# Pacing the last loads and stores of a fused linear-attention and FFN kernel, and moving five q chunks from TensorE transposes to DMA transposes

## The chip, the cores and the metric

The kernel runs on one core of one Trainium2 chip. The metric is the device time of one execution in microseconds (us). Every set of runs also contains runs of the kernel before, taken on the same chip. A run counts as slow when it is over 1.5% above the fastest run of the same kernel in its set; 2% is the threshold for "faster" or "slower".

## The reference

A linear attention with position-dependent features is followed by a feed-forward network (FFN) on all tokens. There are 8 batches, 8 heads, 576 positions and a head size of 64, so 4608 tokens of width 512.

```python
def phi(x, c, s):                       # 64 -> 128 features
    r = np.maximum(x, 0.0)
    return np.concatenate([r * c, r * s], axis=-1)
q_p, k_p = phi(q, cos_w, sin_w), phi(k, cos_w, sin_w)
kv  = np.einsum('bhsf,bhsd->bhfd', k_p, v)
z   = np.sum(k_p, axis=2)
num = np.einsum('bhsf,bhfd->bhsd', q_p, kv)
den = np.einsum('bhsf,bhf->bhs', q_p, z)[..., None] + 1e-06
x   = (num / den)                       # -> (4608, 512)
out = ((x @ w1) * (x @ w2) @ w3) @ w_out
```

## The kernel before

The kernel multiplies w3 and w_out once (`w34b`), and then works through the tokens in nine tiles of 512, t = 0 to 8. A tile is 24 *steps*, each of four wide matmuls: sixteen steps of products with w1 and w2, whose elementwise product is `abT`, and eight of output, which read it. The attention of later batches is slipped between these steps as narrow work. A batch has five chunks of rows. For each of them the kernel makes the q features, transposes them (`qpT`), multiplies them with `kvs` (called *num* here), normalizes the result (`xblk`), and transposes that into `xT`, which the FFN tile reads. So there are two transposes. Each can be done by TensorE, with a copy out of PSUM, or by a DMA that SP (SyncE) issues:

```python
def order_of(b):
    return [0, 1, 2, 3, 4] if b % 2 == 0 else [4, 0, 1, 2, 3]

def dma_q(b):                 # the q chunks that the DMA transposes
    return order_of(b)[5 if b < 2 else 2 if b == 2 else 0:]

def prep_q(b, c):
    features(b, feat_of(b)[1], raw[b, "q"], c)
    if c in dma_q(b):
        R = ROWS[c]
        nc.sync.dma_start_transpose(out=att_of(b)["qpT"][:, :, ds(columns_of(b, c), R)],
                                    in_=feat[b][1][:R, c].rearrange("p h f -> p (h f)"))
# ... (num, normalize) ...
def x_tr(b, c, by_vector=False, pst=None):
    # ...
    if b >= 2:
        nc.sync.dma_start_transpose(out=xT[t][:, :, ds(o, R)], in_=xf)
        return
    # ... else four transposes on TensorE and a copy
```

GpSimd issues the loads and most stores. The results of tiles 1 to 4 are held in SBUF in pairs of 512 KB, eight pairs, and stored in tiles 5 and 6. The other pairs are stored when they are made.

```python
held_pool.append(ctx.enter_context(tc.tile_pool(name="held", bufs=8)))

def store_held():
    osb, g = held.pop(0)
    store(nc.gpsimd, osb[:, :, :], g, 2)
# ... the plan of the tiles, cut:
    else:
        if t + 1 < B:
            attention_at(t + 1, slots, kv=(0, 1, 2, 3, 4), tr=(2, 4, 7, 10, 13),
                         nu=(6, 8, 10, 12, 14), xt=(6, 8, 10, 12, 14))
        for g in {5: (3, 9, 15, 20), 6: (1, 6, 11, 16)}.get(t, ()):
            slots[g].append(store_held)
        if t + 2 < B:
            spread(interleaved(t + 2), 0, 22, slots)
```

## Time and profile before

| | before |
|---|---|
| time, median of 3 | 251.24 us (251.13 to 251.31) |
| TensorE (PE) busy | 242.9 us of a span of 249.5 |
| VectorE (DVE), ScalarE (ACT), GpSimd (POOL) busy | 141.6, 124.5, 90.9 us |
| granted TensorE clock | full in every slice |
| waits of PE after 23 us | none listed |

The span is what the profiler sees of one execution; the device time is about 1.8 us longer. The prediction shows the lines of the page and reads them.

### The profile page before, as it was taken

What the parts mean: (1) busy time and instruction counts of PE and PEld (TensorE: products, weight loads), DVE (VectorE), ACT (ScalarE), POOL (GpSimd) and SP (SyncE); (2) the same over time, 40 slices, a digit from 0 to 9 for tenths busy, and PEclk for the clock granted to TensorE, in tenths of its full rate; (3) what the DMA queues carried; (4) which work ended last, traced back from release to release, by engine and by line L of the source; (5) the groups of instructions that cost most, each with busy time, mean ns of one, the idle gap of its engine ahead of it and who ended that gap; (6) DMA issues with size and microseconds to landing.
All of it is one profiled execution on the core that took longest, in us unless ns stands there. A gap on an engine that the chain in (4) does not pass through costs nothing.

```text
span 249.5 us, 4973 instructions
## 1 busy us (share of the span) xinstructions
PE 242.9 (97%) x1879; PEld 130.2 (52%) x1879; DVE 141.6 (57%) x338; ACT 124.5 (50%) x209; POOL 90.9 (36%) x171
## 2 busy tenths in 40 slices
PE   8899999999999999999999999999999999999994
PEld 3478555666555455545545554555455544444443
DVE  7876665657889628905980695189227704312321
ACT  2676325925966656555655555555432242323320
POOL 7754254540533612441433326280365040023000
PEclk9999999999999999999999999999999999999999
DMA  6999999999999999999999989999798992014013
GB/s 191 183 194 199 209 204 205 198 199 198 267 133 172 170 202 158 156 181 125 160 107 206 189 100 191 190 184 159 107 203 254 240 146 65 3 32 137 1 44 127
DMA packets 80760, 39.85 MB, mean 160 GB/s; under 512 B 48224, under 2 KB 77280, under 8 KB 80736
## 3 DMA queue, kind: packets, MB, share of 16 engines
q0 software_dynamic: 37024, 27.20, 72.0%
q1 hardware_dynamic: 43280, 11.87, 31.9%
q10 hardware_dynamic: 432, 0.46, 0.5%
q8 instruction: 15, 0.25, 0.4%
q14 instruction: 9, 0.07, 0.1%
HBM read 38.80 MB, written 9.44 MB: 193 GB/s over the span
## 4 chain that ended last, share of the span: by engine, by line
PE 92%; DMA 3%; DVE 1%; issue 1%; POOL 1%; ACT 0%; POOLq 0%
PE ffnps L462 50%; PE ffnps L508 24%; PE ffnps L230 6%; PE pnum L353 4%; PE pnum L295 4%; DMA qs<-in_q_dram 3%; PE pst L326 2%; PE pst L218 1%; PE pst L390 1%; PE ffnps L531 1%; POOL vs L112 0%; DVE xblk L363 0%; PE pfirst L353 0%; ACT xT L392 0%; DVE qp L263 0%
## 5 line engine op out<-in xcount | busy, mean ns | idle before, releaser
L503 DVE TENSOR_TENSOR abT<-asb,ffnps 128x512 bf16<-128x512 bf16 x68 | 46.5, 683 | 71.4 <-PE ffnps L462 70.6
L462 PE MATMUL ffnps<-xT,w1b 128*128 128x512 bf16 (+2 forms) x320 | 74.9, 357 | 0.4 <-ACT xT L392 0.2
L462 PE MATMUL ffnps<-xT,w2b 128*128 128x512 bf16 (+2 forms) x320 | 74.9, 357 | 0.0
L499 ACT CAST asb<-ffnps 128x512 bf16<-128x512 f32 x68 | 39.8, 586 | 61.6 <-PE ffnps L462 56.0
L508 PE MATMUL ffnps<-w34b,abT 128*128 128x512 bf16 x280 | 63.0, 379 | 0.0
L462 PEld LDWEIGHTS <-w1b 128*128 128x128 bf16 x320 | 29.4, 98 | 29.6 <-issue 0.6
L508 PEld LDWEIGHTS <-abT 128*128 128x128 bf16 x280 | 26.9, 98 | 31.1
L462 PEld LDWEIGHTS <-w2b 128*128 128x128 bf16 x320 | 26.8, 98 | 20.3
L267 ACT ACTIVATE qp<-qs,sinv 128x512 bf16<-128x512 bf16 (+2 forms) x40 | 28.3, 717 | 1.6 <-DMA qs<-in_q_dram 1.6
L363 DVE TENSOR_TENSOR xblk<-pnum,den 128x512 bf16<-128x512 f32 (+1 forms) x39 | 26.9, 691 | 1.4
L436 POOL DMA_DIRECT2D out_dram<-osb x20 | 10.6, 535 | 46.0 <-ACT osb L518 46.0
L287 POOL COPY va<-vs 128x512 bf16<-128x512 bf16 (+1 forms) x30 | 18.4, 624 | 18.7 <-PE pnum L295 8.9
L267 ACT ACTIVATE kp<-ks,sinv 128x512 bf16<-128x512 bf16 (+1 forms) x35 | 24.7, 721 | 0.0
L518 ACT COPY osb<-ffnps 128x512 f32<-128x512 f32 x19 | 11.1, 585 | 21.9 <-PE ffnps L508 21.9
L353 PEld LDWEIGHTS <-qpT 128*128 128x128 bf16 x320 | 15.1, 98 | 8.6 <-DVE qpT L340 0.6
L263 DVE TENSOR_SCALAR qp<-qs,cosv 128x512 bf16<-128x512 bf16 (+1 forms) x40 | 16.5, 418 | 0.7 <-DMA qs<-in_q_dram 0.6
L295 PEld LDWEIGHTS <-kp 128*128 128x128 bf16 x280 | 13.1, 98 | 7.1
L518 ACT COPY held<-ffnps 128x512 f32<-128x512 f32 x16 | 9.4, 586 | 14.3 <-PE ffnps L508 14.3
L353 PE MATMUL pnum<-kvs,qpT 128*128 128x65 bf16 x312 | 16.5, 194 | 0.0
L544 POOL COPY seen<-kp 128x1 bf16<-128x1 bf16 (+1 forms) x20 | 3.8, 188 | 33.9 <-DVE kp L263 26.1
L230 PE MATMUL ffnps<-woutb,w3T 128*128 128x512 bf16 x64 | 15.4, 379 | 0.0
L295 PE MATMUL pnum<-va,kp 128*128 128x65 bf16 x280 | 14.1, 193 | 0.0
(88 smaller groups left out, 195.3 us busy)
## 6 DMA issues: line engine op xcount, KB each, us to landing
out_dram<-held POOLq DMA_DIRECT2D x10, 256.0 KB, 6.3
qs<-in_q_dram POOLq DMA_DIRECT2D x8, 256.0 KB, 7.9
w3b<-in_moe_w_dram POOLq DMA_DIRECT2D x8, 256.0 KB, 12.8
ks<-in_k_dram POOLq DMA_DIRECT2D x6, 320.0 KB, 10.9
qs<-in_q_dram POOLq DMA_DIRECT2D x6, 320.0 KB, 8.6
vs<-in_v_dram POOLq DMA_DIRECT2D x6, 320.0 KB, 9.0
ks<-in_k_dram POOLq DMA_DIRECT2D x6, 256.0 KB, 8.2
vs<-in_v_dram POOLq DMA_DIRECT2D x6, 256.0 KB, 10.9
```

The costliest lines, as they stand in the source:

```text
L230: nc.tensor.matmul(acc[:, :], lhsT=w3T[:, lc, :], rhs=woutb[:, lc, :], start=(lc == 0), stop=(lc == 7))
L263: nc.vector.tensor_scalar(out=dst[:R, c, :, 0:D], in0=src[:R, :, c, :], scalar1=0.0, scalar2=cosv[:R, at:at + 1], op0=ALU.max, op1=ALU.mult)
L267: nc.scalar.activation(out=dst[:R, c, 0:n, D:F], in_=src[:R, 0:n, c, :], func=ACTF.Relu, scale=sinv[:R, at:at + 1], bias=0.0)
L287: eng.tensor_copy(out=feat_of(b)[2][:R, c, :, 0:D], in_=raw[b, "v"][:R, :, c, :])
L295: nc.tensor.matmul(kvt[:, h // 4, ds((h % 4) * 65, 65)], lhsT=kp[:, c, h, :], rhs=va[:, c, h, 0:D + 1], start=(i == 0 and h % 4 == 0), sto ...
L353: nc.tensor.matmul(nt[:, h // 4, ds((h % 4) * 65, 65)], lhsT=qpT[:, h, ds(at, 128)], rhs=kvs[:, h, :], start=True, stop=True)
L363: nc.vector.tensor_tensor(out=xblk[rows], in0=n4[:, :, :, 0:D], in1=den[rows].unsqueeze(3).to_broadcast([R, 2, 4, D]), op=ALU.mult)
L462: nc.tensor.matmul(out, lhsT=w[:, kc, ts(jc, 128)], rhs=x[:, kc, tok], start=(kc == 0), stop=(kc == 3))
L499: nc.scalar.copy(out=asb[:], in_=aT[:, :])
L503: nc.vector.tensor_mul(out=abT[:, jc, :], in0=asb[:], in1=bT[:, :])
L508: nc.tensor.matmul(ops[:, :], lhsT=abT[:, jc, ts(ms, 128)], rhs=w34b[:, jc, :], start=(jc == 0), stop=(jc == 7))
L518: nc.scalar.copy(out=osb[:, ms % 2, :], in_=ops[:, :])
```

## The change

The intent is to take five of the seven q chunks of batches 1 and 2 that TensorE still transposes over to the DMA, to give up one of the two raw buffers of q and v, and to pace all work of a batch on fixed steps, 25 steps apart. The SBUF that this frees holds twelve output pairs instead of eight. No pair is stored before the last batch: ten pairs are stored behind the steps of batch 7, each issued by GpSimd after it has read one column of what that step wrote, and six at fixed steps after that.

```diff
+    def raw_tile(name):
+        return ld.tile([P, H, NCH, D], BF16, name=name + "s", bufs=2 if name == "k" else 1)
@@
-        load(2, "kqv")
@@
-        return order_of(b)[5 if b < 2 else 2 if b == 2 else 0:]
+        return order_of(b)[5 if b == 0 else 2 if b == 1 else 0:]
@@
-        held_pool.append(ctx.enter_context(tc.tile_pool(name="held", bufs=8)))
+        held_pool.append(ctx.enter_context(tc.tile_pool(name="held", bufs=12)))
@@ (the old load_piece and interleaved are gone)
+    def behind(ap, *what):
+        seen = sm.tile([P, 1], BF16, name="seen", bufs=1)
+        nc.gpsimd.tensor_copy(out=seen[0:64, :], in_=ap)
+        if what:
+            load(*what)
+        else:
+            store_held()
@@ (behind_k, behind_q, behind_x: behind() of one column of k features, q features, x)
+    def plan_batch(b):
+        z = 28 + 25 * (b - 2)
         for i, c in enumerate(order_of(b)):
+            plan[z - 9 + 3 * i // 2].append(lambda c=c: prep_k(b, c))
+            if b + 1 < B and i in (0, 2):
+                plan[z - 9 + 3 * i // 2].append(lambda i=i: behind_k(b, i, b + 1, "k", i // 2))
+            plan[z - 5 + i].append(lambda c=c: prep_v(b, c))
+            g = z - (2 if b == 2 else 4) + 2 * i
+            plan[g].append(lambda c=c: prep_q(b, c))
+            if b == B - 1:
+                plan[g].append(lambda i=i: behind_q(b, i))
+            if b + 1 < B and i in (2, 4):
+                plan[g].append(lambda i=i: behind_q(b, i, b + 1, "v", i // 4))
+            plan[z + 1 + i].append(lambda c=c, i=i: kv_chunk(b, c, i))
+            plan[z + 7 + 2 * i].append(lambda c=c: num(b, c))
+            if b + 1 < B and i in (1, 3):
+                plan[z + 7 + 2 * i].append(lambda i=i: behind_x(b, i, b + 1, "q", i // 2))
+            if b == B - 1:
+                plan[z + 7 + 2 * i].append(lambda i=i: behind_x(b, i))
+            plan[z + 7 + 2 * i].append(lambda c=c: x_tr(b, c))
@@
+    for g in (170, 172, 174, 176, 192, 194):
+        plan[g].append(store_held)
@@ (batch 1)
-            attention_at(1, between, kv=(14, 14, 14, 14, 15), tr=(12, 13, 17, 18, 19),
-                         nu=(16, 17, 18, 20, 22), xt=(18, 19, 20, 22, 25))
+            attention_at(1, between, kv=(14, 14, 14, 14, 14), tr=(12, 13, 17, 18, 19),
+                         nu=(15, 17, 19, 20, 25), xt=(18, 20, 21, 22, 27))
+            for i in range(2):
+                between[11 + i].append(lambda i=i: behind_q(1, 2 + 2 * i, 2, "k", i))
+            for i, g in enumerate((15, 17, 17, 19)):
+                between[g].append(lambda i=i: behind_x(1, (i + 1) // 2, 2, "vvqq"[i], i % 2))
```

For batch 7, z is 153. Its q features and q transposes come at steps 149 to 157, each with a store behind it; its num and x at 160 to 168, again each with a store. Tile 7 begins at step 168.

More of the change, by code (lines that the diff above doesn't have):

```diff
@@ L108, with load_first @@
     raw = {}
-    def load_first(eng, t, src, c0=0, n=4, b=0):
-        rows = src[b, :, 0:512, :].rearrange("h (p j) d -> p h j d", j=4)
-        eng.dma_start(out=t[:, :, c0:c0 + n, :].rearrange("p h j d -> p h (j d)"),
-                      in_=rows[:, :, c0:c0 + n, :].rearrange("p h j d -> p h (j d)"))
+    def load_first(eng, t, src, c0=0, n=4, b=0, rows=slice(0, P)):
+        at = src[b, :, 0:512, :].rearrange("h (p j) d -> p h j d", j=4)
+        eng.dma_start(out=t[rows, :, c0:c0 + n, :].rearrange("p h j d -> p h (j d)"),
+                      in_=at[rows, :, c0:c0 + n, :].rearrange("p h j d -> p h (j d)"))
     def load_first4(eng, t, src, b=0):
         eng.dma_start(out=t[0:64, :, 4, :], in_=src[b, :, 512:S, :].rearrange("h p d -> p h d"))
+    def raw_tile(name):
+        return ld.tile([P, H, NCH, D], BF16, name=name + "s", bufs=2 if name == "k" else 1)
     def load(b, which, part=None):
@@ L121, in load @@
             if part != 1:
-                raw[b, name] = ld.tile([P, H, NCH, D], BF16, name=name + "s")
+                raw[b, name] = raw_tile(name)
             if b in own:
-                if part != 1:
-                    load_first(nc.gpsimd, raw[b, name], src, b=b)
-                if part != 0:
+                half = slice(64 * part, 64 * part + 64)
+                load_first(nc.gpsimd, raw[b, name], src, b=b, rows=half)
+                if part == 1:
                     load_first4(nc.gpsimd, raw[b, name], src, b=b)
@@ L149 @@
     k0 = raw[0, "k"] = wst.tile([P, H, NCH, D], FP32, name="kf", bufs=1)
-    q0 = raw[0, "q"] = ld.tile([P, H, NCH, D], BF16, name="qs")
-    v0 = raw[0, "v"] = ld.tile([P, H, NCH, D], BF16, name="vs")
+    q0 = raw[0, "q"] = raw_tile("q")
+    v0 = raw[0, "v"] = raw_tile("v")
     load_first(nc.sync, k0, k)
@@ L512, in ffn_groups @@
             if ms % 2 == 0:
-                if 1 <= t <= 4:
-                    osb = held_pool[0].tile([P, 2, 512], FP32, name="held")
-                else:
-                    pool = (fsb, held_pool[0])[ms // 2]
-                    osb = pool.tile([P, 2, 512], FP32, name="osb", bufs=1)
+                osb = held_pool[0].tile([P, 2, 512], FP32, name="held")
             nc.scalar.copy(out=osb[:, ms % 2, :], in_=ops[:, :])
@@ L520, in ffn_groups @@
                 store((nc.sync, nc.scalar)[ms % 2], osb[:, ms % 2:ms % 2 + 1, :], 4 * t + ms, 1)
-            elif ms % 2 == 1 and 1 <= t <= 4:
+            elif ms % 2 == 1:
                 held.append((osb, 4 * t + ms - 1))
-            elif ms % 2 == 1:
-                store(nc.gpsimd, osb[:, :, :], 4 * t + ms - 1, 2)
             yield
@@ L539, in prep_units @@
         return [(lambda f=f, c=c: f(b, c)) for f in parts for c in order_of(b)]
-    def load_piece(b, i, dst, c):
+    def behind(ap, *what):
         seen = sm.tile([P, 1], BF16, name="seen", bufs=1)
-        nc.gpsimd.tensor_copy(out=seen[0:ROWS[c], :], in_=dst[0:ROWS[c], c, 0, 0:1])
-        load(b, "kqv"[i // 2], i % 2)
-    def interleaved(b, pieces=range(5)):
-        units = []
-        for i, c in enumerate(order_of(b)):
-            units.append(lambda c=c: prep_k(b, c))
-            if b + 1 < B:
-                units.append(lambda c=c, i=i: load_piece(b + 1, pieces[i], feat[b][0], c))
-            units.append(lambda c=c: prep_q(b, c))
-            if b + 1 < B and i == NCH - 1 and pieces[i] < 5:
-                units.append(lambda c=c: load_piece(b + 1, 5, feat[b][1], c))
-            units.append(lambda c=c: prep_v(b, c))
-        return units
+        nc.gpsimd.tensor_copy(out=seen[0:64, :], in_=ap)
[3 more added lines that the diff above has]
+            store_held()
@@ new lines, in behind_k, with behind_q, behind_x @@
+    def behind_k(b, i, *what):
+        behind(feat[b][0][0:64, order_of(b)[i], 0, 0:1], *what)
+    def behind_q(b, i, *what):
+        behind(feat[b][1][0:64, order_of(b)[i], 0, 0:1], *what)
+    def behind_x(b, i, *what):
+        c = order_of(b)[i]
+        r = out_rows(b, c).start
+        behind(att[b]["x"][c][r:r + 64, 0, 0, 0:1], *what)
+    plan = [[] for _ in range(24 * NT)]
+    def plan_batch(b):
+        z = 28 + 25 * (b - 2)
+        for i, c in enumerate(order_of(b)):
+            plan[z - 9 + 3 * i // 2].append(lambda c=c: prep_k(b, c))
[15 more added lines that the diff above has]
+            plan[z + 7 + 2 * i].append(lambda c=c: x_tr(b, c))
@@ L594 @@
                                                      space=bass.MemoryType.PSUM)))
+    for b in range(2, B):
+        plan_batch(b)
+    for g in (170, 172, 174, 176, 192, 194):
+        plan[g].append(store_held)
     for t in range(NT):
@@ L611 @@
             between = [[] for _ in range(32)]
-            later = [[] for _ in range(24)]
             spread(prep_units(1, (prep_k,)), 6, 8, between)
@@ L615 @@
             spread(prep_units(1, (prep_v,)), 13, 13, between)
-            attention_at(1, between, kv=(14, 14, 14, 14, 15), tr=(12, 13, 17, 18, 19),
-                         nu=(16, 17, 18, 20, 22), xt=(18, 19, 20, 22, 25))
-            later[:8] = between[24:32]
+            attention_at(1, between, kv=(14, 14, 14, 14, 14), tr=(12, 13, 17, 18, 19),
+                         nu=(15, 17, 19, 20, 25), xt=(18, 20, 21, 22, 27))
+            later = between[24:32]
+            for i in range(2):
+                between[11 + i].append(lambda i=i: behind_q(1, 2 + 2 * i, 2, "k", i))
+            for i, g in enumerate((15, 17, 17, 19)):
+                between[g].append(lambda i=i: behind_x(1, (i + 1) // 2, 2, "vvqq"[i], i % 2))
             for jp in range(8):
@@ L627 @@
             slots[16].append(open_held)
-            slots[16].append(lambda: load(3, "kqv"))
-            spread(prep_units(2, (prep_k,)), 20, 23, slots)
         elif t == 1:
-            for g in range(24):
-                slots[g] += later[g]
-            spread(prep_units(2, (prep_q,)), 0, 4, slots)
-            spread(prep_units(2, (prep_v,)), 0, 4, slots)
-            attention_at(2, slots, kv=(2, 3, 4, 5, 6), tr=(3, 5, 7, 9, 11),
-                         nu=(8, 10, 12, 14, 16), xt=(8, 10, 12, 14, 16))
-            slots[4].append(lambda: load_piece(4, 0, feat[2][1], 3))
-            spread(interleaved(3, range(1, 6)), 6, 23, slots)
-        else:
-            if t + 1 < B:
-                attention_at(t + 1, slots, kv=(0, 1, 2, 3, 4), tr=(2, 4, 7, 10, 13),
-                             nu=(6, 8, 10, 12, 14), xt=(6, 8, 10, 12, 14))
-            for g in {5: (3, 9, 15, 20), 6: (1, 6, 11, 16)}.get(t, ()):
-                slots[g].append(store_held)
-            if t + 2 < B:
-                spread(interleaved(t + 2), 0, 22, slots)
+            for g, units in enumerate(later):
+                slots[g] += units
+        for g in range(24):
+            slots[g] += plan[24 * t + g]
         for g, _ in enumerate(ffn_groups(t)):
```

## The prediction

> **What bounds the kernel now.** I read the page first: its row of engines, the slices, and the chain of work that ended last.
>
> ```profile
> PE 242.9 (97%) x1879; PEld 130.2 (52%) x1879; DVE 141.6 (57%) x338; ACT 124.5 (50%) x209; POOL 90.9 (36%) x171
> ...
> PE   8899999999999999999999999999999999999994
> ...
> PEclk9999999999999999999999999999999999999999
> ...
> PE 92%; DMA 3%; DVE 1%; issue 1%; POOL 1%; ACT 0%; POOLq 0%
> ```
>
> TensorE is busy in every slice, at full clock, and 92% of the chain lies on it; the next engine, VectorE, is at 57%. But a PE that is "busy" may still be waiting inside, since the ends of its matmuls are modelled, so I checked two things. The waits of PE are these, all of them:
>
> ```profile
> PE unread L180 <- DVE zeros L156: 1.2, 1, 1.2
> PE kva L312 <- DVE va L287: 0.9, 1, 0.9
> PE ffnps L462 <- ACT xT L392: 0.2, 1, 0.2
> PE pst L339 <- DVE qp L263: 0.2, 1, 0.2
> PE ffnps L462 <- DVE xT L392: 0.2, 1, 0.2
> ```
>
> 2.7 us, all before 23 us. The second check is by start times in the timeline of PE, where the next start, not the duration, gives the cost:
>
> ```profile
> 47.06 1.03 PE L230 MATMUL ffnps<-woutb,w3T 128*128 128x512 bf16 x4
> 47.92 0.61 PE L326 MATMUL pst<-identb,qp 128*128 128x128 bf16 x8
> 48.37 1.03 PE L230 MATMUL ffnps<-woutb,w3T 128*128 128x512 bf16 x4
> ...
> 53.89 1.02 PE L508 MATMUL ffnps<-w34b,abT 128*128 128x512 bf16 x4
> 54.75 0.61 PE L326 MATMUL pst<-identb,qp 128*128 128x128 bf16 x8
> 55.25 0.43 PE L353 MATMUL pnum<-kvs,qpT 128*128 128x65 bf16 x8
> ...
> 59.92 0.39 PE L390 MATMUL pst<-identb,xblk 128*128 128x128 bf16 x4
> 60.14 0.42 PE L353 MATMUL pnum<-kvs,qpT 128*128 128x65 bf16 x8
> 60.40 1.89 PE L508 MATMUL ffnps<-w34b,abT 128*128 128x512 bf16 x8
> ```
>
> Four wide matmuls (one "step" of the FFN; a token tile has 24) cost 47.92-47.06 = 0.86 us. Eight transposes of q, one chunk, cost 48.37-47.92 = 0.45 us. Four of x cost 0.22, eight narrow matmuls (one chunk of kv or of num) 0.26 us. With these I recompute a stage. Tiles 2 to 6 last from 88.03 to 204.45 = 116.42 us, 23.28 each; the work is 24 x 0.864 = 20.74 plus ten narrow chunks at 0.255 = 2.55, together 23.29. Tiles 7 and 8 begin at 204.45 and 225.17, 20.72 apart, which is 24 x 0.864. So from 88 us to the end PE has no gap at all: nothing that moves loads, copies or stores about can gain there. It can only lose.
>
> **What the Trainium skill says.** "TensorE: Matmul & The Clock Gate", section "Part 4: PE-mode transpose", gives about 275 ns per 128x128 transpose in a kernel and names the copy out of PSUM that follows. The trace differs on what a transpose costs the stream: its row shows 219 ns each, but eight start within 0.45 us, 56 ns apiece; I use that. "PSUM — Partial Sum Buffer", section "Engine vs sequencer instructions": the queues of ScalarE, VectorE and GpSimd are strict FIFO. So a feature step that waits for its q load stands in front of the abT product behind it; the trace of before has only 0.6 us of such waiting on VectorE for q and does not test it. "DMA: Bandwidth & Descriptors", section "Issuing engines are not separate DMA queues": SP's transposes and GpSimd's loads interleave on the same 16 engines. The landing times of before fit that: x transposes take from 2.4 to 9.6 us, q transposes from 3.2 to 11.3.
>
> ```profile
> L385 SPq DMA_TRANSPOSE xT<-xblk x30: 1171/1218/3447, 75.3 to 199.3; - x30
> DMA to landing us min/median/max: 2.4/5.4/9.6
> ...
> L281 SPq DMA_TRANSPOSE qpT<-qp x28: 1194/1280/3884, 68.5 to 179.9; - x28
> DMA to landing us min/median/max: 3.2/6.2/11.3
> ```
>
> **The change part by part.** I counted the instructions on each engine in the order of both programs.
>
> (1) PE loses exactly 40 matmuls, 1879 to 1839, all of them q transposes: three chunks of batch 1 and two of batch 2, which now go through the DMA transpose. The first two chunks of batch 1 stay on PE. 5 x 0.445 = 2.2 us, wholly on the path, since three lie between 52.7 and 63.5 us and two in tile 1, both PE-bound. VectorE loses their five copies, 5 x 0.69 = 3.4 us, off the path.
>
> (2) The stage from 52.68 to 63.47 us is 10.79 us long. Its work: eight steps 6.91, five num chunks 1.28, three q chunks 1.33, x transposes 0.11 + 3 x 0.22 = 0.77, sum 10.29. So 0.5 us is small waits; by start times they are 0.09 us before the first num, 0.06 before the second, 0.10 before the first x transpose and 0.22 after it. In the changed order the transposes of q no longer share the two PSUM transpose buffers here, num of batch 1 begins at 15 instead of 16, and most num and x transposes have an FFN step of 0.86 us between them. I count 0.4 us of the 0.5 as gained. Tile 1 has another 24.56-24.41 = 0.15 us, of which I count nothing. One num chunk moves from tile 0 into tile 1: zero.
>
> (3) Loads. Batch 2 no longer loads at 40 to 47 us but behind the features and products of batch 1 (about 46 to 59 us); q and v have one raw buffer each. All later loads are spread over the tile. None is on PE; the gain is zero, the risk is under the rivals.
>
> (4) Twelve output pairs held (before eight), all sixteen pairs stored from step 149 on: ten behind the q features and x of batch 7, six at fixed steps. Same bytes, no PE work. The last two pairs go at steps 192 and 194, about where tile 7's stores ran before (201.9 to 226.6 us covers tiles 6 and 7), so the tail of the last tile, 244.16 to 249.5 us, stays.
>
> (5) GpSimd gets 47 one-column copies instead of 25, 22 more at 0.19 us = 4 us, on an engine at 36%: nothing.
>
> Sum: 251.24 - 2.2 - 0.4 = 248.6 us if no new wait appears.
>
> **The rivals.** *First, the x transposes come too late for their tile.* Before, tile t+1's batch had its products at steps 6 to 14 of tile t; now a batch is paced every 25 steps, and the x that a tile needs is produced only eight or nine steps ahead of it. For tile 3 the last needed num stands at step 64 and the tile begins at 72: seven steps and two num chunks, 7 x 0.864 + 2 x 0.26 = 6.6 us. For tiles 5 and 7 three chunks lie between: 6.8 us. For tiles 2, 4 and 6 there are nine steps, about 7.4, 7.7 and 8.0 us. From this comes off the normalization, 0.16 + 0.20 + 0.69 = 1.05 us, and some 0.3 us in VectorE's and SP's queues. That leaves 5.2 us against a median landing of 5.4: right on the edge. For it: the old maximum of 9.6 us. Against it: that median comes from x transposes queued between q transposes and loads; now q transposes end before the x begin, loads are paced singly, and 2.4 to 4 us should be usual. If each of tiles 2 to 7 stalled by 1 us, six tiles eat 6 us: 254.6. I expect one or two stalls of some tenths.
>
> *Second, the stores collide with batch 7.* Ten pairs of 512 KB start within steps 149 to 168, about 20 us, which is 5.2 MB or some 260 GB/s, with the transposes of q and x of batch 7 in the same time; the slices of before peak at 267 GB/s. The x that tile 7 waits for is issued at step 160, behind five pairs. If it lands in 8 us instead of 5, PE stalls 2 to 3 us once. Against it: queues interleave, and GpSimd itself waits when its transfers are outstanding (it waited 4.5 us in all for held stores before).
>
> *Third, q of batch 2.* Its second half is issued behind x of order 2, whose num ends by my sums at 57.0 us; plus 1.1 us of VectorE and GpSimd's two issues of 0.68, it leaves near 59 us. Its first feature stands at step 26, which PE reaches near 64.5 us. Loads took 4.5/7.9/11.6 us to land before; with the burst of 40 to 55 us gone I expect 5 to 7, so VectorE and ScalarE wait 0 to 1.5 us. PE can run some four steps on through the four FFN tiles in PSUM, so it stalls only if q lands after about 67.3 us: not likely, worth 0 to 1 us.
>
> *Fourth, a larger gain.* PE's work bounds it: with the start and tail kept, at most 2.2 us of work and the 0.65 us of waits just named go. 248.3 is the floor; 2% would need 246.2.
>
> **Range and chances.** Base 248.6; I add 0.4 us for the average of the first three rivals: 249.0. Low end 248.2, just under the floor for spread between runs (251.13 to 251.31 before). High end 250.9, where stalls cost 2.3 us over the base. For slower by over 2%, 256.3 us, stalls would have to reach 7.7 us, more than 1 us at every tile: 3%. Faster by over 2%: 1%. The rest within.
>
> **What would show it.** Right: PE with 1839 instructions, busy near 240 us; the stage of the eight output steps of tile 0 about 2 us shorter; PE's list of waits still under 4 us; tiles 2 to 6 still 23.3 us each. First rival: waits of L464 products on the transposes into xT at the starts of tiles, tiles longer than 23.3, and x landings near 5 us or more. Second: such a wait at tile 7 alone, with landings of x of 8 us and stores round it. Third: VectorE waiting for the load of qs near 65 us with a gap on PE near 68. My prediction is wrong if PE gets idle by more than 2 us in tiles 1 to 7, or if the stage around 53 to 63 us does not shrink.

## More of the kernel before

The features of batch t+2, with their q transposes, are made during tile t, a whole tile before their num. And x of batch t+1 is made at steps 6 to 14 of tile t, so the first x transpose has 18 steps (24 - 6), about 15.6 us, before tile t+1 reads it.

## The result, and the profile after

The changed kernel took 261.32 us (258.95 to 263.75), the kernel before 251.28 in the same set. Ratios in this document are the mean time of one kernel's fast runs over the mean of the other's in the same rounds, so they are not quite the ratio of the quoted medians. Here the ratio is 1.036 (95% interval 1.029 to 1.044): slower. The prediction was 249.0 us with a range of 248.2 to 250.9.

The profiled run of that set was the slowest of the four and counts as slow, so the same kernel was run once more (e10_changed_again below, 258.92 us for the profiled run, fast). Both profiles have the same stall at the same place; all detailed readings are from the fast one. This is the page of the slow one, its row of engines, slices of PE and of the clock, and the chain:

```profile
PE 243.6 (93%) x1839; PEld 127.7 (49%) x1839; DVE 142.9 (55%) x333; ACT 123.1 (47%) x209; POOL 95.7 (37%) x196
...
PE   8799999999999999999999999999998129999995
...
PEclk9999999999999999999999999999999757999999
...
PE 82%; DMA 13%; issue 2%; DVE 1%; POOL 1%; ACT 0%; POOLq 0%
```

PE did lose 40 matmuls, and the slices before the hole are nearly as full as before. Line numbers have moved by two: L464 is the product with w1 or w2, L510 the output, L355 num, L387 the DMA transpose of x. The hole takes about two slices of 6.5 us, the 32nd and 33rd; in them and in the next one the clock is granted at 0.5 to 0.7. The share of DMA in the chain has gone from 3% to 13%. The hole is the start of tile 7. The list of PE's waits in the fast profile (in all, times, longest) begins:

```profile
PE ffnps L464 <- issue: 5.7, 1, 5.7
PE pnum L355 <- DMA qpT<-qp: 1.5, 1, 1.5
```

In the slow profile the first two are 9.2 and 2.4 us. Here is PE's timeline of the fast profile at that place (start, duration, instruction, wait before it and what ended it):

```profile
203.42 0.43 PE L355 MATMUL pnum<-kvs,qpT 128*128 128x65 bf16 x8 [1.47 <-DMA qpT<-qp]
203.69 1.02 PE L510 MATMUL ffnps<-w34b,abT 128*128 128x512 bf16 x4
210.39 1.87 PE L464 MATMUL ffnps<-xT,w1b 128*128 128x512 bf16 x4 [5.68 <-issue]
212.05 0.65 PE L355 MATMUL pnum<-kvs,qpT 128*128 128x65 bf16 x8
212.51 1.72 PE L464 MATMUL ffnps<-xT,w2b 128*128 128x512 bf16 x4
214.06 1.03 PE L464 MATMUL ffnps<-xT,w1b 128*128 128x512 bf16 x4
```

A num waits 1.47 us for its transposed q. Then the first product of tile 7, which reads `xT`, waits 5.68 us. "Issue" means that the profile could not name what it waited for; SP's timeline of the same profile names it:

```profile
186.42 14.07 SPq L283 DMA_TRANSPOSE qpT<-qp  x5
200.59 14.55 SPq L387 DMA_TRANSPOSE xT<-xblk  x5
```

The first block of x was normalized by 197.4 us, but SP was still issuing q transposes until 200.49. The first x transpose was issued at 200.59 and landed after 9.7 us, the longest of its kind in this stretch, so at 210.3 us. PE goes on at 210.39.

After the hole, four wide matmuls take 212.05 - 210.39 = 1.66 us instead of 0.86, eight narrow ones 0.46 instead of 0.26, and four more wide ones 1.55; from 214.06 on it is 0.86 again. The half speed costs 0.80 + 0.20 + 0.69 = 1.7 us. The view by windows shows it (the columns after the window are its length, busy time and instructions of PE, PEld, DVE, ACT and POOL, then the clock, the DMA share and GB/s):

```profile
208.00:212.00 4.00, 1.61 (x4) 0.59 (x5) 0.00 (x0) 0.00 (x0) 1.06 (x2) 0.50 1.15 320
```

The clock is at 0.50 while the DMA engines move 320 GB/s. The Trainium skill, "TensorE: Matmul & The Clock Gate", section "What's actually happening", states that the clock falls to half after an idle window of about 3.4 us and comes back after about 3.4 us of sustained work. The trace agrees on the second figure: work resumes at 210.39 and the clock is whole again 3.7 us later. On the first it differs: PE is idle from 204.7 on, and in windows of 1 us the clock is down from 207 on, after 2.3 us. PE had also stood still for 1.47 us shortly before, so that it worked for only 1.3 of the 5.1 us up to the fall.

Where the time went, by the starts of the tiles in PE's timelines (us). The last column is the version of e1b_stores_away_gated below, which has the change without the stall:

| | before | changed (fast profile) | stores moved away |
|---|---|---|---|
| tile 1 begins | 63.47 | 62.22 | 61.75 |
| tile 2 begins | 87.87 | 86.44 | 85.97 |
| tile 6 begins | 181.00 | 179.88 | 179.53 |
| tile 7 begins | 204.28 | 210.39 | 202.55 |
| tile 8 begins | 225.00 | 233.05 | 223.52 |
| end of the span | 249.5 | 257.1 | 247.5 |

Up to tile 6 the change gained 1.12 us. Tile 6 then lasted 30.51 instead of 23.28 us; the difference of 7.23 is the two waits, 1.47 + 5.68 = 7.15. Tile 7 lasted 22.66 instead of 20.72, that is 1.94 more: 1.7 of half speed, and one num chunk of 0.26 that now lies in it. The last tile took 24.05 instead of 24.5 us, a gain of 0.45 that was not looked into.

### The profile page after: what moved, and what is told of

Read it like the earlier page. It is cut to its first block, busy times and chain, and to the rows that moved or that the text cites. A ratio compares the mean times of both kernels' runs of the same rounds, so it can differ in the third digit from the quotient of the medians.

```text
span 261.9 us, 4941 instructions
## 1 busy us (share of the span) xinstructions
PE 243.6 (93%) x1839; PEld 127.7 (49%) x1839; DVE 142.9 (55%) x333; ACT 123.1 (47%) x209; POOL 95.7 (37%) x196
## 4 chain that ended last, share of the span: by engine, by line
PE 82%; DMA 13%; issue 2%; DVE 1%; POOL 1%; ACT 0%; POOLq 0%
PE ffnps L464 47%; PE ffnps L510 18%; DMA qpT<-qp 10%; PE ffnps L232 5%; PE pnum L355 3%; PE pnum L297 3%; DMA qs<-in_q_dram 3%; PE pst L220 1%; PE pst L392 1%; PE pst L328 1%; PE ffnps L527 1%; DVE xblk L365 1%; POOL vs L112 0%; PE pfirst L355 0%; ACT xT L394 0%
## 5 line engine op out<-in xcount | busy, mean ns | idle before, releaser
L464 PE MATMUL ffnps<-xT,w1b 128*128 128x512 bf16 (+2 forms) x320 | 76.1, 362 | 9.5 <-issue 9.2
L464 PE MATMUL ffnps<-xT,w2b 128*128 128x512 bf16 (+2 forms) x320 | 75.8, 361 | 0.0
L510 PE MATMUL ffnps<-w34b,abT 128*128 128x512 bf16 x280 | 65.9, 379 | 0.0
L464 PEld LDWEIGHTS <-w1b 128*128 128x128 bf16 x320 | 29.1, 98 | 38.0 <-issue 11.8
L516 ACT COPY held<-ffnps 128x512 f32<-128x512 f32 x35 | 20.5, 585 | 51.9 <-PE ffnps L510 51.9
L464 PEld LDWEIGHTS <-w2b 128*128 128x128 bf16 x320 | 28.9, 98 | 27.2 <-issue 0.6
L510 PEld LDWEIGHTS <-abT 128*128 128x128 bf16 x280 | 25.5, 98 | 26.2
L438 POOL DMA_DIRECT2D out_dram<-held x42 | 22.1, 532 | 21.1 <-DMA out_dram<-held 10.4
L269 ACT ACTIVATE kp<-ks,sinv 128x512 bf16<-128x512 bf16 (+1 forms) x35 | 24.5, 721 | 0.0
L363 DVE TENSOR_SCALAR den<-pnum 128x8 f32<-128x8 f32 (+1 forms) x39 | 6.4, 165 | 32.7 <-PE pnum L355 32.7
L355 PEld LDWEIGHTS <-qpT 128*128 128x128 bf16 x320 | 15.0, 99 | 13.8 <-issue 3.7
L540 POOL COPY seen<-xblk 64x1 bf16<-64x1 bf16 x19 | 3.5, 185 | 46.4 <-DVE xblk L365 46.4
L265 DVE TENSOR_SCALAR qp<-qs,cosv 128x512 bf16<-128x512 bf16 (+1 forms) x40 | 18.7, 473 | 1.0 <-DMA qs<-in_q_dram 1.0
L355 PE MATMUL pnum<-kvs,qpT 128*128 128x65 bf16 x312 | 16.7, 195 | 2.6 <-DMA qpT<-qp 2.4
L289 POOL COPY va<-vs 128x512 bf16<-128x512 bf16 (+1 forms) x30 | 17.5, 630 | 0.0
L540 POOL COPY seen<-qp 64x1 bf16<-64x1 bf16 x17 | 3.3, 191 | 38.9 <-DVE qp L265 38.9
```

The lines of the kernel that those rows point to most:

```text
L265: nc.vector.tensor_scalar(out=dst[:R, c, :, 0:D], in0=src[:R, :, c, :], scalar1=0.0, scalar2=cosv[:R, at:at + 1], op0=ALU.max, op1=ALU.mult)
L269: nc.scalar.activation(out=dst[:R, c, 0:n, D:F], in_=src[:R, 0:n, c, :], func=ACTF.Relu, scale=sinv[:R, at:at + 1], bias=0.0)
L355: nc.tensor.matmul(nt[:, h // 4, ds((h % 4) * 65, 65)], lhsT=qpT[:, h, ds(at, 128)], rhs=kvs[:, h, :], start=True, stop=True)
L438: eng.dma_start(out=rows[:, :, cols], in_=osb[64 * i:64 * i + rows.shape[0], :, cols])
L464: nc.tensor.matmul(out, lhsT=w[:, kc, ts(jc, 128)], rhs=x[:, kc, tok], start=(kc == 0), stop=(kc == 3))
L510: nc.tensor.matmul(ops[:, :], lhsT=abT[:, jc, ts(ms, 128)], rhs=w34b[:, jc, :], start=(jc == 0), stop=(jc == 7))
```

## The experiments

The leading theory, called A in some of the texts: the pairs stored behind batch 7's q features and x delay, in the DMA engines, the transposes of q and x that batch 7 needs at once. Its main rivals: the lead of eight steps is too short in any case (then removing stores would not help, and an earlier batch 7 would); the late load of batch 2 or the single raw buffers do the harm; or, as a finer form of A, it is not the bytes that count but how packets of two queues take turns (T in the texts). Edits are against the changed kernel unless said otherwise.

### e1_stores_away: the stores after batch 7's transposes, first try

```diff
-            if b == B - 1:
-                plan[g].append(lambda i=i: behind_q(b, i))
...
-            if b == B - 1:
+            if b < B - 1 and i == 4:
                 plan[z + 7 + 2 * i].append(lambda i=i: behind_x(b, i))
...
-    for g in (170, 172, 174, 176, 192, 194):
+    for g in (170, 172, 174, 176, 178, 180, 182, 184, 186, 192, 194):
```

> The changed kernel with its stores moved, nothing else: five pairs go singly behind the last products of batches 2 to 6, the other eleven from step 170 on, when no transpose is left that a near product waits for. Theory A (the ten pairs stored beside batch 7 hold up its DMA transposes, and PE waits for them): the waits of 2.2 and 9.2 us at 204 to 215 us and the slow clock after them (about 2 us) go, and the first part's lead stays: 249 to 250.5 us. Rival B (the pace of 25 steps, with x made only eight steps ahead of tile 7, is too tight whatever else moves): a wait of several us stays at the start of tile 7, 255 us or more.

Measured: 263.54 us, ratio 1.039 (1.036 to 1.042). No faster than the changed kernel (ratios 1.036 and, in e10, 1.038): a miss. The cause is in the edit. The late stores had nothing to wait for, and a step number orders only the instructions of one engine; GpSimd, which had no other work, ran ahead and issued them in a burst. Its timeline shows this:

```profile
188.19 4.83 POOL L438 DMA_DIRECT2D out_dram<-held  x9
```

Instead of after 200 us they ran beside batch 7's q transposes, and PE waited again: in its profile (a slow run) 7.2 us at tile 7 and 6.3 us in four waits on `qpT`. What follows: the edit did not test what it was meant to. With stores again beside the transposes the stall was there, as A says; that the waits sum to more than in the changed kernel's slow profile (13.5 against 11.6 us) proves nothing, since the fast runs of the two do not differ.

### e2_half_stores: three pairs behind q, two behind x

```diff
-            if b == B - 1:
+            if b == B - 1 and i % 2 == 0:        # behind q features
...
-            if b == B - 1:
+            if b == B - 1 and i % 2 == 1:        # behind x
...
+    for g in (170, 172, 174, 176, 178, 180, 182, 184, 186, 192, 194):
```

> Five of the ten pairs stay beside batch 7 (behind q features 0, 2, 4 and products 1, 3), five go to steps after 170. Theory A, with lateness that grows with the stores in the way: landings of batch 7's last q transposes and first x transpose of some 6 to 9 us instead of 12.9 to 16.8, PE waits of 2 to 5 us in all instead of 11.4, 252 to 256 us. Rival B: no change beyond noise, about 260 us.

Measured: 249.70 us, ratio 0.993 (0.991 to 0.995). The stall is gone altogether: no wait of PE is listed after 59 us, and batch 7's q transposes landed in 3.2/4.3/7.3 us (minimum, median, maximum). This is better than I had expected; half the stores did not give half the stall, they gave none. The lead of eight steps was left as it was, so it is not too short by itself.

### e4_pe_last_batch: all stores in place, the critical transposes back on TensorE

```diff
     def dma_q(b):
+        if b == B - 1:
+            return order_of(b)[:3]
...
-        if b >= 2:
+        if b >= 2 and (b, c) != (B - 1, 4):                  # x transposes by DMA
...
-            plan[z + 7 + 2 * i].append(lambda c=c: x_tr(b, c))
+            if b == B - 1 and i >= 3:
+                plan[z + 2 * i - 1].append(lambda c=c: q_tr(b, c))
+            plan[z + (10 if b == B - 1 and i == 0 else 7 + 2 * i)].append(lambda c=c: x_tr(b, c))
```

> All stores where the changed kernel has them; only the three transposes of batch 7 with a near deadline (its last two q chunks, its first x block) go back to TensorE. Theory A says that PE stood still for late DMA transposes and nothing else: no wait over 1 us is left, 2 x 0.45 + 0.11 = 1.0 us of PE work comes back, 250 to 251.5 us. If instead the stores slow PE, VectorE or the buffers themselves (rival C), most of the 10 us stays: 257 us or more.

Measured: 251.29 us, ratio 0.999 (0.997 to 1.001). With every store where the change had put it, taking the first x block and the last two q chunks of batch 7 off the DMA removes the stall; the longest wait after the start of the kernel is 0.3 us on `qpT`. So the stores harm PE only through these transposes. The repair costs PE two q chunks and a small x chunk, 2 x 0.445 + 0.11 = 1.0 us. That is the larger part of the 1.6 us by which e4 lies above e2 in the same set, and it ends level with the kernel before; the rest was not followed up.

### e5_q_by_dma_alone: the kernel before, with only the q chunks moved

```diff
-        return order_of(b)[5 if b < 2 else 2 if b == 2 else 0:]
+        return order_of(b)[5 if b == 0 else 2 if b == 1 else 0:]
```

> The kernel before with one line changed: five q chunks of batches 1 and 2 go through the DMA transpose, loads, pace and stores as before. If the gain of the first part of the change is just PE work removed: 251.2 - 2.2 = 249.0 us, up to 0.4 less for small waits. If it needs the paced loads (the burst of loads at 40 to 55 us delays these transposes), a new wait eats it: 250.5 us or more.

Measured: 257.34 us, ratio 1.024 (1.021 to 1.026): slower. Without the paced loads, the part of the change that should gain loses 6 us. PE waits three times for `qpT`, 4.9 us in all. The view of that tile up to 62 us (SP's issues with their durations in ns, and the landings) shows why:

```profile
L281 SPq DMA_TRANSPOSE qpT<-qp x3: 1333/4560/4696, 48.5 to 54.6; - x3
...
DMA to landing us min/median/max: 10.6/13.7/13.7
```

The q transposes of batch 1 run here beside the loads of batches 2 and 3, which themselves land after 15 to 17 us. So the moved transposes need the rest of the change. The landings point to the moved loads as the part that they need, but no run moved the loads alone, so this is not shown by itself.

### e1b_stores_away_gated: the stores after batch 7's transposes, done properly

The edit is that of e1, but each late store now waits for one column of the FFN products of its step, so that GpSimd cannot run ahead:

```diff
-        abT = fsb.tile([P, 8, 512], BF16, name="abT", bufs=2)
+        abT = abTs[t] = fsb.tile([P, 8, 512], BF16, name="abT", bufs=2)
...
+    def behind_ab(g):
+        t, r = divmod(g, 24)
+        behind(abTs[t][0:64, min(7, max(0, r // 2 - 1)), 0:1])
...
-    for g in (170, 172, 174, 176, 192, 194):
-        plan[g].append(store_held)
+    for g in (170, 172, 174, 176, 178, 180, 182, 184, 186, 194, 196):
+        plan[g].append(lambda g=g: behind_ab(g))
```

Five pairs go singly, one behind the last x of each of batches 2 to 6; eleven from step 170 on.

> The earlier attempt to take the stores away left its eleven late ones without anything to wait for, so GpSimd issued them at 188 us, beside batch 7, and made it worse (263.5 us). Here each of them waits for a column of the abT product of its own step, from step 170 on. Theory A (stores beside batch 7 delay its DMA transposes): no PE wait over 1 us after 180 us, last q and first x transpose of batch 7 land in under 7 us, 249 to 250.3 us. Rival B (the pace alone is too tight): 255 us or more.

Measured: 249.56 us, ratio 0.991 (0.987 to 0.996). This is the best version, level with e2 and e8, and it beats both kernels, though the gain over the kernel before is under 2%. The kernel before was restless in this set (250.8 to 252.7), so I compare with its 251.28 of the first set: 1.7 us. E2 gives 1.7 us too, within its own calm set. In e1b's profile the q transposes of batch 7 are issued and land like this (issue durations in ns, then landings in us):

```profile
L283 SPq DMA_TRANSPOSE qpT<-qp x5: 1194/1231/1233, 186.5 to 193.7; - x5
...
DMA to landing us min/median/max: 2.7/3.1/3.3
```

Here are the same lines of the changed kernel in its fast profile:

```profile
L283 SPq DMA_TRANSPOSE qpT<-qp x5: 1196/1720/4239, 186.4 to 196.3; - x5
...
DMA to landing us min/median/max: 3.2/6.3/12.0
```

Two things differ. The transposes land later, and even the issue of one takes up to 4.2 us instead of 1.2. SP issues in order, so the x transposes stand behind it: the first is issued at 197.12 in e1b, at 200.59 in the changed kernel.

### e3a_split_rows and e3b_split_512B: the same stores in other pieces

```diff
+            # e3a: each store of GpSimd as two halves of the rows
+            half = rows.shape[0] // 2
+            for s in range(2):
+                eng.dma_start(out=to[half * s:half * s + half], in_=of[half * s:half * s + half])
+            # e3b: as two DMAs of alternating pieces of 512 bytes
+            to, of = (ap.rearrange("p j (a b m) -> p b (j a) m", a=2, b=2) for ap in (to, of))
+            for s in range(2):
+                eng.dma_start(out=to[:, s], in_=of[:, s])
```

> The changed kernel with every GpSimd store cut in two by rows: twice as many issues, same bytes, same pieces of 2 and 4 KB. It is the control for the next run. Stall like the changed kernel's: 257 to 264 us; if the doubled issue time of GpSimd alone spreads the stores enough, less, and the next run must be read against this one.

> As the run before it, the same issues and bytes, but every store is cut into alternating pieces of 512 bytes. If a transpose waits its turn behind each store packet (theory T: turns, so the size of the packet counts), its packets of some 250 bytes pass sooner: landings in batch 7 under 9 us, 3 us or more faster than the control. If only the bytes in flight count (theory S: share of bandwidth), the same time as the control or longer[...].

Measured: 253.86 us, ratio 1.006 (1.000 to 1.013), and 254.73 us, ratio 1.008 (1.002 to 1.015). Both are much better than the changed kernel and nearly equal. Twice as many issues, with a wait of 2.0 us for earlier stores among them, spread the same bytes over more time: the five pairs behind q go out from 187.35 to 204.87 us in e3a's profile, a fast run, so within 17.5 us instead of 11.2. The run of rows, meant as the control, thus already removed most of the stall. The turn-taking of packets was not put to the test: from 186 to 216 us the store queue's packets still averaged 3.61 MB / 1440 = 2.5 KB with pieces of 512 bytes (e3b's profile, a slow run), against 4.43 MB / 1739 = 2.5 KB in the control. The Trainium skill, "DMA: Bandwidth & Descriptors", section "Queues, rings and completion order", states that each DMA engine goes round its queues by the packet. In the changed kernel the packets are very unequal, as the DMA view of 186 to 212 us shows (store queue, then transpose queue: packets, MB, share):

```profile
q0 software_dynamic: 1345, 4.21, 53.7%
q1 hardware_dynamic: 5883, 1.45, 50.1%
```

That is 3.1 KB a packet for the stores and 246 bytes for the transposes. If turns are taken by the packet, large packets on the other queue would delay small ones much; no run here shows whether this is the mechanism, nor whether the profile's packets are those of the page, and it stays open.

### e6_away_more_dma: e1b with one more q chunk and one x block by DMA

```diff
-        return order_of(b)[5 if b == 0 else 2 if b == 1 else 0:]
+        return order_of(b)[5 if b == 0 else 1 if b == 1 else 0:]
...
-        if b >= 2:
+        if b >= 2 or (b, c) == (1, 3):
```

> The gated version with one more q chunk and one x block of batch 1 moved from TensorE to the DMA transpose: 0.45 + 0.22 = 0.67 us of PE work less. If these land in time, 0.5 to 0.7 us faster than the gated version; if the q chunk (needed some 7 us after its features) comes late, a wait of up to 2 us at num of batch 1 near 54 us and no gain.

Measured: 252.19 us, ratio 1.001 (0.998 to 1.005). Worse than e1b by 2.6 us in the same set. PE waits four times on `qpT`, 2.7 us in all, the first until 52.67 us. So the two moves together do not pay here; which of them cost how much, this run does not tell.

### e7_batch7_sooner: all of batch 7 four steps earlier, stores unchanged

```diff
-        z = 28 + 25 * (b - 2)
+        z = 28 + 25 * (b - 2) - (4 if b == B - 1 else 0)
```

> The changed kernel with batch 7's whole plan, its stores included, four steps (3.5 us) earlier; the stores stand to the transposes as before, only tile 7 is further off. If the short lead is the other half of the cause, the wait at tile 7 shrinks by what the four steps and the chunks among them take, 3.5 to 4.5 us, some of the slow clock with it: 255 to 258 us. If only the stores count, or the earlier features wait for q and stop PE themselves: 259 us or more.

Measured: 259.30 us, ratio 1.029 (1.021 to 1.037). This is slower than I had expected. The wait at the start of tile 7 is gone, but others have come in its place, and the half clock with them:

```profile
PE pnum L355 <- DMA qpT<-qp: 5.2, 3, 2.8
PE ffnps L464 <- ACT asb L501: 1.3, 1, 1.3
```

Num comes as many steps after its q transpose as before, so it now waits on `qpT`, with q landing in a median of 8.0 us. The second line has another cause, which the expectation named too: ScalarE waited 3.1 us for the load of q at the earlier features, the work for `asb` stood behind that, and PE stopped for 1.27 us at 186 us. More lead for the last link of the chain is no cure while the first link is delayed by the same stores.

### e8_eight_pairs and e9_q_pairs_only: which stores

```diff
 # e8: three pairs behind q features, all five behind x
-            if b == B - 1:
+            if b == B - 1 and i % 2 == 0:        # behind q features
+    for g in (170, 172, 174, 176, 178, 180, 192, 194):

 # e9: all five pairs behind q features, one behind x (the last)
-            if b == B - 1:
+            if b == B - 1 and i == 4:            # behind x
+    for g in (170, 172, 174, 176, 178, 180, 182, 184, 192, 194):
```

> Eight of the ten pairs stay beside batch 7: three behind q features 0, 2, 4 as in the run with half the stores, and all five behind the products. If what counts are the stores ahead of the transposes that tile 7 and its num wait for, the three of five make the difference and this is near the run with five pairs: 249.7 to 251.5 us. If the delay grows with all stores in the window, eight of ten give most of the 10 us: 255 us or more.

> The complement of the run with eight pairs: all five pairs behind the q features of batch 7 stay, the four behind its first four products go to after its last product. If the five in a row behind the q features are what delays the transposes, the waits stay: last q chunk or first x block lands after 9 us or more, 254 to 261 us. If it takes the stores behind the products as well, no wait over 1 us: 249.5 to 251 us.

Measured: e8 249.57 us, ratio 0.992 (0.989 to 0.994), and e9 256.46 us, ratio 1.015 (1.007 to 1.023), which is unclear against 2%. Against e8 the direction is plain: the slowest of e8's runs took 250.37 us, the fastest of e9's 252.80. E9's profiled run counts as slow, but it is like its two fast runs of 256.45 and 256.48. Its first wait stands at the first product of tile 7, which reads `xT`, although the view names `qpT`:

```profile
PE ffnps L464 <- DMA qpT<-qp: 3.8, 1, 3.8
```

In e9 the q transposes of batch 7 landed in 3.2/6.8/12.0 us, in e8 in 3.2/4.2/5.6. So it is the five pairs in a row behind the q features that do most of the harm. These are their issues in GpSimd's timeline of the changed kernel, fast profile:

```profile
187.02 0.58 POOL L438 DMA_DIRECT2D out_dram<-held  x1 [0.43 <-issue]
...
189.07 0.55 POOL L438 DMA_DIRECT2D out_dram<-held  x1
...
191.54 2.13 POOL L438 DMA_DIRECT2D out_dram<-held  x4 [0.28 <-issue]
...
197.16 1.04 POOL L438 DMA_DIRECT2D out_dram<-held  x2 [1.01 <-DMA out_dram<-held]
```

Each pair is 512 KB in one, two or four DMAs. The first five pairs, 2.6 MB, are issued within 11.2 us from 187.0 on (the fourth, at 193.9, and the first half of the fifth, at 195.1, are left out here; the last line is the second half of the fifth), which asks for some 235 GB/s while the q transposes run. With three in the same time, as in e8, it is some 140 GB/s, and PE's list has no wait for `qpT`. The first issue held back because earlier stores are still under way, by 1.0 us, is that second half of the fifth pair; that brake comes after the harm. The five behind x are harmless if those behind q are three: in e8 batch 7's x landed in 5.8/7.7/9.5 us, and PE's list has one wait of 0.2 us for it. The record also shows how much the transpose queue moved from 187 to 197 us: 1.18 MB in e1b, 0.94 in e8, 0.66 in the changed kernel. The packets of the two queues together took 62.5% of the 16 engines' time in e1b and 97% in both others.

### e10_changed_again: the changed kernel once more

No edit.

> The changed kernel itself, unchanged. Its only profile fell in a run called slow (263.75 us, over 1.5% above its fastest), so every reading of it might be of that state. If the waits for batch 7's transposes are what makes it slow at all, a run of the fast state shows the same waits, smaller: 6 to 10 us in all at 200 to 215 us, one drop of the granted clock after them, and 257 to 263 us. If the slow run had another cause, a fast profile shows none of these waits.

Measured: 260.08 us, ratio 1.038 (1.032 to 1.044). It confirms the first result and gives the fast profile that is read above. The runs spread from 258.92 to 262.57, and the clock averages from 0.987 down to 0.974 with them, so that longer runs have more time at half clock. The clock is here a result of the stall and not its cause: in the fast profile it falls near 207 us, after PE has stopped at 204.7.

## Why the prediction was wrong

**What bounds the kernel: right.** TensorE at full clock bounds it, and "nothing that moves loads, copies or stores about can gain there. It can only lose" is what happened after 88 us.

**Step (1), 40 matmuls less, 2.2 us: right in the count, with less of the gain in hand.** Counted from the same matmul near 22.5 us (22.55 before, 22.68 in the fast profile, 22.22 in e1b), tile 2 comes 1.56 us sooner than before in the fast profile and 1.57 in e1b. What else separates these two in the table is the start of the kernel, where the fast profile waits 0.8 us for `va` and e1b does not. So some 0.65 of the 2.2 us were lost in gaps before narrow chunks. Tile 1 should now last 24 x 0.864 + eleven narrow chunks at 0.255 + 0.22 = 23.77 us and lasts 24.22. Before, it had no gap: the prediction's 0.15 us there comes from taking the two ends of the tile, 63.47 and 88.03, from two views; in the timeline tile 2 begins at 87.87, so tile 1 lasted 24.40. The list of the weight loads' waits in the fast profile, for 62 to 88 us, begins with the cause of part of it:

```profile
PEld L355 <- DMA qpT<-qp: 0.9, 2, 0.5
```

Num of batch 2 now depends on q transposes by DMA that are barely in time. Most of the 0.9 us lies beside matmuls; the rest is part of the 0.45 us of gaps.

**Step (2), 0.4 us of small waits gained: wrong.** The stage from the first num to tile 1 lasts 62.22 - 52.90 = 9.32 us, and its work, by the prediction's own durations, 6.91 + four num chunks 1.02 + 0.77 of x transposes = 8.70. So 0.62 us are gaps, and 0.10 more stand before the first num (52.80 to 52.90); counted the same way, 0.5 were there before. Instead of 0.4 gained, 0.2 were lost. The largest gap is new; it is in the timeline of the fast profile:

```profile
58.31 0.39 PE L392 MATMUL pst<-identb,xblk 128*128 128x128 bf16 x4
58.92 0.42 PE L355 MATMUL pnum<-kvs,qpT 128*128 128x65 bf16 x8 [0.23 <-DVE xblk L365]
```

Num starts 0.61 us after the x transposes, which need 0.22, since it waits for VectorE's normalization. With the gaps of tile 1, the gain without a stall is 1.7 us (e1b, e2 and e8 at 249.6) and not the 2.6 of the sum.

**Step (3), loads, "the gain is zero": wrong in what it left out.** No run shows that moving the loads gains by itself, but in the old plan, with the loads where they were, step (1) costs 6 us (e5).

**Step (4), stores, "no PE work": the step that failed, together with the second rival.** Twelve held pairs and the burst in batch 7 do no PE work, and the whole loss comes from them all the same: e2, e8 and e1b take the stores out of the way and reach 249.6, e4 keeps them and takes the transposes out of the way. The rival was named rightly ("the stores collide with batch 7"), with even the rate of 260 GB/s, but was given "PE stalls 2 to 3 us once" and a small chance. Three terms of its sum were missing or too small:

- It looked at one landing, that of x. The q transposes in front of it collide first. They delayed a num by 1.47 us, and kept SP busy until 200.5 us, so that x was issued 3.2 us after it was ready.
- x landed after 9.7 us where the rival had 8. With the late issue, the wait at tile 7 was 5.68 us, and the waits together 7.15 instead of 2 to 3.
- A stall of this length halves the clock afterwards: 1.7 us more.

The sum for the fast profile: 251.28 - 1.12 (up to tile 6) + 7.23 (tile 6) + 1.94 (tile 7) - 0.45 (last tile) = 258.88, measured 258.92. Other runs have longer stalls (in the slow profile 9.2 + 2.4 us of waits), which makes 261.3 the median.

**The argument against that rival failed, too.** "Queues interleave" is true (the Trainium skill's section on issuing engines, which the prediction named, and the two queues in the packets above), but it says nothing about shares; with both queues active, q transposes went from a median of 3.1 to 6.3 us. "GpSimd itself waits when its transfers are outstanding" is true as well, but the first such wait comes in the middle of the fifth pair.

**The first rival: hardly there.** Tiles 2 to 5 together last 179.88 - 86.44 = 93.44 us against 93.13 before, 0.3 us in all. Eight steps of lead are enough where no stores are about, which is what made tile 7 look safe: the landings that I read off the kernel before (median 5.4) belonged to a plan with 18 steps of lead, in which a landing of 9.6 us cost nothing. **The third rival** hardly showed: q of batch 2 landed in 6.7 to 7.0 us, ScalarE waited 0.55 us for it near 66 us, and on PE it can at most be part of the small gaps of tile 1. **The fourth,** the floor of 248.3, was not reached by any version.

## What to carry to other kernels

When a plan is tightened so that a transfer has just enough time, list every transfer that will be under way in that window and how many bytes they ask for; a landing time read from a plan with slack is not one for a plan without. Moving work from the bounding engine to DMA paid here only where no burst of loads (e5) or stores (e9) ran beside the moved transposes. Each late link also delayed what was queued behind it and, after 2 to 3 us of idleness in most cases, halved TensorE's clock. A position in program order does not hold back an engine with nothing else to do: a store that is to come late has to wait for data that comes late.

## What the Trainium skill lacked or had wrong

- "DMA: Bandwidth & Descriptors", section "Latency and other measured facts", gives DMA transposes a bandwidth (261 GB/s in one kernel) but no time to land, alone or beside other traffic. Here q chunks of 256 KB (128 x 1024 in bf16; one of a batch's five is half as large) landed after a median of 3.1 us on a quiet path (e1b), 6.3 and up to 12.0 beside 2.6 MB of stores issued within 11.2 us (changed kernel), and 13.7 beside loads that took 15 to 17 us (e5).
- The same page has nothing on the issue of a DMA transpose growing longer under load: 1.2 us each in e1b, up to 4.2 in the changed kernel. On SP this delays every later transpose.
- The same page states turn-taking by the packet between queues, but not what it means for small packets beside large ones. The store queue had 3.1 KB a packet and the transpose queue 246 bytes; whether that is the cause was not settled by e3a and e3b.
- "TensorE: Matmul & The Clock Gate", section "What's actually happening": "after ≥1 idle window (~3.4µs)" is too mild as a guide for how long PE may stand still. In the changed kernel the clock fell 2.3 us after PE stopped. In e5 a wait of 2.16 us, and in e7 one of 2.80 us, were followed by a clock near half (0.54 for 60 to 62 us, 0.50 for 208 to 211), while another wait of 2.27 us in e5 was not (1.00). The page's free-running window fits that the outcome varies. The time back to full clock agrees: 3.7 us.
- The same page, section "Part 4: PE-mode transpose", gives about 275 ns per transpose; here one lasts 219 ns in its row and eight in a row cost the stream 56 ns each, as the prediction already noted.
